# One transfer per quad and per stored tile, two stores for the last tile, and another table of product counts, in a fused attention and feed-forward kernel

## The chip, the cores and the metric

The kernel runs on one core of a Trainium2 chip. The metric is device time in microseconds (us) of one execution; lower is better. In the profile, PE is the matrix engine (PEld its weight loads), ACT the scalar engine, DVE the vector engine, POOL the general engine, and SP the engine that here only issues transfers; SPq, ACTq and POOLq are the queues of transfer instructions that SP, ACT and POOL issue. Sixteen DMA engines move the data of all these queues.

## The reference

Eight batches, 12 heads, 448 positions of 64 numbers. Queries and keys are divided by their norms, attention is taken with a temperature of 0.1, and the result, laid out as 3584 tokens of 768 numbers, goes through a feed-forward layer with `h * cos(h)` between its two products.

```
q_n = q / (norm(q, axis=-1) + 1e-06)
k_n = k / (norm(k, axis=-1) + 1e-06)
scores = q_n @ k_n.transpose(0, 1, 3, 2) / tau          # tau = 0.1
attn = softmax(scores)
x = (attn @ v).transpose(0, 2, 1, 3).reshape(3584, 768)
h = x @ w_in                                            # 768 x 2048
out = (h * cos(h)) @ w_out                              # 2048 x 768
```

Inputs and output are float32. The kernel gives its matrix products bfloat16 operands.

## The kernel before

**Quads and batches.** Attention is done in 24 quads; a quad is four heads of one batch, so three quads (numbers 3b, 3b+1, 3b+2) make batch b. For a quad, `load_qk` brings Q and K in (SP), `square` and `inverse` take the inverse norms, `scale` divides (POOL or DVE), and `turn` transposes Q and K with two transfers (SP). `scores` makes 7 groups of score products (line 549), ACT takes their exponentials (line 556), and `attend` multiplies them with V (line 566). The sum over the keys is applied afterwards. For quads 6 to 23 this goes two quads at a time, in what the code calls a round (`ROUNDS`, `sums`, `invert`): PE sums the exponentials of both quads (line 629), ACT takes the logarithm and the negative exponential of the sums (lines 645 and 647), which leaves eight distinct rows of 448 inverse sums, and ACT sends these eight rows to a scratch tensor in memory, `rscr` (line 648). SP then fetches them back, spread over partitions, into a tile `R` (line 654): for each quad two transfers, one for partitions 0 to 63 and one for 64 to 127. Every partition of a half receives the same 896 numbers. POOL multiplies the attention result with `R` and writes the bfloat16 tile `xT` (line 657). `R` has two buffers, used in turn by quads.

**Batch products.** When the three quads of a batch are in `xT`, PE makes the first product of the feed-forward layer, 96 matrix instructions (`m1_part`, line 675); ACT and DVE apply `h * cos(h)` (`m1`, lines 688 to 694). Then follow the second products of the output tiles that this batch completes (`m2`, line 703). A tile t is 128 tokens; there are 28 tiles. Each has two halves of 384 columns, 16 instructions each; DVE copies each half to `osb` (line 711), which has three buffers, and after the second half SP stores the tile with two transfers, of partitions 0 to 63 and of 64 to 127 (line 717). A token's place in the output is such that the 64 tokens of a half stand 7 rows apart, and the two halves start one row apart, except in tiles 3, 10, 17 and 24, whose halves belong to different batches.

**Order.** Between the second products, the attention work of later batches is put in: `VISITS` lists, for each batch, pairs (slots of attention to do, second products to do after them), and `LATER` shifts the place of a quad's `attend` among its slots. PE executes in the order in which the code creates its operations. The other engines' order comes from `Planner`, which runs through a list of estimated durations once, at build time, and emits a fixed order for each engine; a transfer's estimate is `dur` on its issuing engine and `moves` for the data. Up to quad 3 (`P.strict`) the order of ACT, DVE and POOL is the order of creation. SP issues its transfers strictly in that emitted order, and an instruction that has to wait holds up those behind it.

Of the kernel before, what the change touches and what calls it, by code (L numbers as in the profile page):

```python
# [16 lines left out]
class Op:  # L17
    __slots__ = ("i", "eng", "dur", "fn", "reads", "writes", "deps", "dma", "lat", "start", "end",
                 "count", "waits", "known", "prio", "moves", "mode", "chain", "behind", "lead", "packet", "lock")


class Planner:
# [20 lines left out]
    def op(self, eng, dur, fn, r=(), w=(), after=(), dma=None, moves=0, mode="f", chain=None, keep=False, lead=0.0,  # L43
           packet=74, lock=False):
        o = Op()
        o.i, o.eng, o.dur, o.fn, o.dma, o.moves, o.mode, o.chain = (
            len(self.ops), eng, dur, fn, dma, moves, mode, chain)
        o.lat = self.FIRST + moves + self.LAST if dma else self.LAT[eng]
        o.behind, o.lead, o.packet, o.lock = None, lead, packet, lock
        if keep or self.strict and eng in ("act", "dve", "pool"):  # L50
            o.behind, self.tail[eng] = self.tail.get(eng), o
# [29 lines left out]

    PASSES, SPREAD = 0, 1.5

    def plan(self):

        rng = random.Random(1)
        shift = [0.0] * len(self.ops)
        least = max(o.end for o in self.pass_(shift))
        for _ in range(self.PASSES):
            n = rng.choice((8, 30, 100))  # L90
            i = rng.randrange(len(shift) - n)
            tried = list(shift)
            for k in range(i, i + n):
                tried[k] += rng.gauss(0.0, self.SPREAD)
            end = max(o.end for o in self.pass_(tried))
            if end <= least:
                least, shift = end, tried
        self.order = self.pass_(shift)
        return self.order

    def pass_(self, shift):
# [11 lines left out]
        t, urge = 0.0, [1e9] * len(ops)  # L113
        for o in ops:
            if o.eng == "pe":
                urge[o.i] = t
                t += o.dur
        later = None
        behind = {}
        for o in reversed(ops):  # L120
            if o.eng == "pe":
                if later is not None:
                    urge[o.i] = min(urge[o.i], urge[later.i] - o.dur)
                later = o
            if o.chain:
# [7 lines left out]
        for o in ops:  # L133
            o.prio = (urge[o.i] if urge[o.i] < 1e8 else 2000.0 + o.i) + shift[o.i] - o.lead
        pe = [o.i for o in ops if o.eng == "pe"]
        pe_next = 0
# [138 lines left out]
def bass_cosine_attention__then__act_gcu_kernel(  # L275
# [42 lines left out]
    sqk = sb("sqk", [128, 2 * NJ, D], BF16)  # L318
    n2 = ring("n2", 2, [128, 4 * NJ], F32)
    nrm = ring("nrm", 2, [128, 4 * NJ], F32)  # L320
    rr = ring("rr", 2, [128, 4 * NJ], F32)
    ne = ring("ne", 2, [128, 4 * NJ, 2], F32)
    Qn = ring("Qn", 1, [128, NJ, 2, D], BF16)
# [38 lines left out]
    for i in range(2):  # L362
        op("dve", 0.1, lambda e, i=i: e.memset(ne[i].ap()[:, :, 1], 1e-6), w=[("eps", i)])

# [65 lines left out]

    def jr(t, w, part, off=0):
        return bass.AP(t, off + w * H + part[0], [[2 * H, 128], [NJ, 2], [1, part[1] - part[0]]])

    def square(qd, w, eng, part=ALL[0], after=()):
# [15 lines left out]
        def add():  # L450
            return op("dve", 0.07 + 0.95 * n, lambda e: e.tensor_reduce(  # L451
                out=n2[u].ap()[:, H * w:H * w + H] if part == ALL[0] else jr(n2[u], w, part),
                in_=dst, axis=AX.X, op=ALU.add),
                r=cut("sq" + nm, 0, part), w=cut("n2%d" % w, u, part))
# [3 lines left out]
    def inverse(qd, w0, w1, part=ALL[0], after=()):  # L458
# [5 lines left out]
        if part == ALL[0]:  # L464
            n = slice(H * w0, H * w1)
            t, z, o = n2[u].ap()[:, n], nrm[u].ap()[:, n], rr[u].ap()[:, n]
        else:
            t, z, o = (jr(a[u], w0, part) for a in (n2, nrm, rr))
        act("exp", 0.12, lambda e: e.activation(z, t, ACT.Ln, bias=1e-30, scale=1.0),
# [3 lines left out]
        if qd == 0:  # L473
# [5 lines left out]
            return  # L479
        two_ = ne[u].ap()[:, H * w0:H * w1]  # L480
        act("exp", 0.12, lambda e: e.activation(two_[:, :, 0], z, ACT.Exp, bias=0.0, scale=0.5), r=x, w=[("ne", u)],
# [5 lines left out]
        op("dve", 0.3, lambda e: e.reciprocal(o, z), r=x, w=y, lead=lead)  # L487

    def scale(qd, w, eng="pool", part=ALL[0]):
        s, u = qd % 3, qd % 2  # L490
        j0, j1 = part
        f, n, nm = ((Qf, Qn, "Q"), (Kf, Kn, "K"))[w]
        rb = bass.AP(rr[u], w * H + j0, [[2 * H, 128], [NJ, 2], [1, j1 - j0], [0, D]])
        return op(eng, (1.05 if eng == "dve" else 1.65) * (j1 - j0) / NJ,
# [14 lines left out]

    def transpose(qd, which, bk, part=ALL[0]):  # L510
        u = qd % 3
# [3 lines left out]
        def mm(e):  # L515
# [6 lines left out]
        src = PS.ap()[:, 512 * bk + 64 * j0:512 * bk + 64 * j1].bitcast(BF16)  # L522
        dst = t[u].ap()[:, j0:j1].rearrange("p j a x -> p (j a x)")
        op("dve", 0.07 + 0.067 * (j1 - j0), lambda e: e.tensor_copy(dst, src), r=whole(bk),  # L524
           w=cut(nm + "T", u, part))
# [112 lines left out]
    def invert(quads, bk):  # L638
# [8 lines left out]
        act("exp", 0.47, lambda e: e.activation(zz, zz, ACT.Exp, bias=0.0, scale=-1.0), r=[("Zs", z)], w=[("Zs", z)], lead=LEAD)  # L647
        op("act", 0.3, lambda e: e.dma_start(rscr.ap()[8 * n:8 * n + rows, :], Zs[z].ap()[0:32 * np_:16, :]),
           r=[("Zs", z)], w=[("rs", n)], dma=("rs", z), moves=0.05, lead=LEAD)
        for i, qd in enumerate(quads):  # L650
            u, sl, b = qd % 2, qd % NA, qd // QB
            for r in range(2):
                ap = bass.AP(rscr, (8 * n + 4 * i + 2 * r) * S, [[0, 64], [S, 2], [1, S]])
                op("sp", 0.6, lambda e, r=r, u=u, ap=ap: e.dma_start(R[u].ap()[64 * r:64 * r + 64], ap),
                   r=[("rs", n)], w=[("R", u, r)], dma=("R", u, r), moves=0.85, packet=140, lead=LEAD)
            c0 = 2 * (qd % QB)
            op("pool", 2.04, lambda e, u=u, sl=sl, b=b, c0=c0: e.tensor_tensor(  # L657
                xT[b % 2].ap()[:, c0:c0 + 2, :], AVs[sl].ap(), R[u].ap(), ALU.mult),
                r=[("AV", sl), ("R", u, 0), ("R", u, 1)], w=[("x", b % 2, qd % QB)], lead=LEAD, lock=True)

# [36 lines left out]
    def m2(t, h, f0, f1, bk):  # L697
# [11 lines left out]
        if f1 == NNB:  # L709
            so = t % 3  # L710
            op("dve", 0.475, lambda e: e.tensor_copy(osb[so].ap()[:, HW * h:HW * h + HW], bank(bk, HW)),  # L711
               r=whole(bk), w=[("o", so, h)])
# [10 lines left out]
    VISITS = [  # L723
# [7 lines left out]
        [],  # L731
        [],
    ]
    LATER = {19: 3, 10: -1, 18: -2, 5: 3, 4: 1, 17: 4, 7: -1, 21: -2, 22: -1, 15: -2, 9: 1}
    E1, E2 = NNB - 6, NNB - 4
# [319 lines left out]
```

## Time and profile before

| | us |
| --- | --- |
| median of three runs | 425.83 (425.01 to 428.05) |
| the profiled execution, its own time | 424.88 |
| its span, from the first to the last instruction | 423.0 |
| PE busy | 406.1 |
| ACT busy | 306.3 |
| DVE busy | 269.5 |
| POOL busy | 200.9 |

The profiled execution ran at the full granted clock (1.00). Its time is 1.88 us more than its span. Stretches that the text uses, from the start of the span: the first product of batch 2 starts at 149.6, that of batch 4 at 245.8, that of batch 7 at 379.7, and the last matrix instruction ends at 418.8. In the groups of the page, a row gives line, engine, operation, destination and source tile, sizes and count, then the busy time and the mean of one instruction, then the idle time of the engine ahead of it. The section on transfers gives the count, the size and the median time from issue to landing. The section on queues gives packets, bytes and the time the packets took as a share of sixteen engines over the span.

### The profile page before, as it was taken

The page shows a single profiled execution, that of the slowest core. Times are in us where ns is not written, and L with a number is a line of the kernel's source. Part 1 is how long each engine was busy: PE and PEld are TensorE (multiplying, and loading weights), DVE is VectorE, ACT ScalarE, POOL GpSimd, SP SyncE. Part 2 cuts the span into 40 slices and gives each one's busy share as a digit, 9 for nine tenths or more (in the row PEclk, how much of TensorE's full clock was granted, in tenths as well). Part 3 has the DMA queues.
Part 4 walks back from the last instruction along what each step waited for, and adds up shares of the span by engine and source line. Part 5 has one row for each costly group of instructions (what it writes and reads, how often), then busy time and mean ns, then how long its engine had stood idle before and what let it go on. Part 6 is the DMA issues. An engine that isn't in the chain of part 4 may idle for free.

```text
span 423.0 us, 8441 instructions
## 1 busy us (share of the span) xinstructions
PE 406.1 (96%) x3586; PEld 212.6 (50%) x3586; DVE 269.5 (64%) x337; ACT 306.3 (72%) x404; POOL 200.9 (47%) x137
## 2 busy tenths in 40 slices
PE   6879998999999999999999999999999999999995
PEld 5345454445544445445555555445554555555563
DVE  5767886879853659733996269824882228736921
ACT  6998689988888977697787677689678656505700
POOL 3566238792387794758628880559213213000000
PEclk9999999999999999999999999999999999999999
DMA  8999997995099969298909990279805523021022
GB/s 272 259 236 209 242 273 165 186 218 135 4 220 227 283 107 251 67 238 212 229 5 211 206 279 2 52 179 177 166 1 82 128 72 92 2 74 39 0 76 74
DMA packets 68230, 62.94 MB, mean 149 GB/s; under 512 B 39961, under 2 KB 60769, under 8 KB 68193
## 3 DMA queue, kind: packets, MB, share of 16 engines
q1 hardware_dynamic: 57808, 50.48, 48.3%
q0 software_dynamic: 10240, 11.80, 16.8%
q8 instruction: 28, 0.46, 0.5%
q10 hardware_dynamic: 144, 0.13, 0.1%
q14 instruction: 10, 0.07, 0.0%
HBM read 53.87 MB, written 11.14 MB: 154 GB/s over the span
## 4 chain that ended last, share of the span: by engine, by line
PE 77%; DMA 12%; ACT 4%; DVE 3%; POOL 2%; issue 0%; ACTq 0%; SPq 0%
PE PS L703 30%; PE PS L675 30%; PE PS L566 7%; PE PS L549 6%; DMA W<-in_moe_w_out_dram 6%; PE PS L629 3%; DMA Kf<-in_k_dram 3%; ACT E L556 2%; DMA R<-rscr 1%; DVE n L451 1%; PE PS L588 1%; DMA rscr<-Zs 1%; DMA Qf<-in_q_dram 1%; DVE osb L711 1%; POOL xT L657 0%
## 5 line engine op out<-in xcount | busy, mean ns | idle before, releaser
L556 ACT ACTIVATE E<-PS 128x896 bf16<-128x896 f32 x168 | 142.4, 919 | 20.8 <-PE PS L549 18.4
L703 PE MATMUL PS<-W,gT 128*128 128x384 bf16 x896 | 157.0, 327 | 0.0
L675 PE MATMUL PS<-xT,W 128*128 128x448 bf16 x768 | 147.0, 353 | 1.3 <-DVE qT L524 1.0
L703 PEld LDWEIGHTS PS<-W,gT 128*128 128x128 bf16 x896 | 82.9, 98 | 69.8 <-issue 15.9
L675 PEld LDWEIGHTS PS<-xT,W 128*128 128x128 bf16 x768 | 74.7, 98 | 71.7 <-DVE qT L524 1.1
L688 ACT ACTIVATE ar<-PS 128x896 int32<-128x896 f32 x64 | 58.2, 911 | 37.5 <-PE PS L675 37.5
L690 DVE SCALAR_TENSOR_TENSOR ar<-ar,PS 128x896 f32<-128x896 int32 x64 | 69.2, 1083 | 22.3 <-ACT ar L688 22.3
L694 DVE TENSOR_TENSOR gT<-PS,ar 128x896 bf16<-128x896 f32 x64 | 69.5, 1088 | 7.5 <-ACT ar L692 7.1
L692 ACT ACTIVATE ar<-ar 128x896 f32<-128x896 f32 x64 | 60.6, 946 | 18.2 <-DVE ar L690 18.0
L711 DVE COPY osb<-PS 128x384 f32<-128x384 f32 x56 | 31.1, 556 | 61.2 <-PE PS L703 60.5
L657 POOL TENSOR_TENSOR xT<-AVs,R 128x896 bf16<-128x896 f32 x18 | 37.4, 2086 | 49.6 <-DMA R<-rscr 49.6
L549 PE MATMUL PS<-qT,kT 64*64 64x448 bf16 x672 | 49.7, 359 | 5.3 <-ACT E L556 2.8
L447 POOL TENSOR_TENSOR sqq<-Qf 128x896 bf16<-128x896 f32 x22 | 36.9, 1677 | 34.0 <-DVE n L451 14.4
L447 POOL TENSOR_TENSOR sqk<-Kf 128x896 bf16<-128x896 f32 x21 | 36.9, 1756 | 33.2 <-DVE n L451 32.0
L495 POOL TENSOR_TENSOR Qn<-Qf,rr 128x896 bf16<-128x896 f32 x21 | 38.0, 1812 | 24.3 <-DVE rr L487 16.7
L575 DVE COPY AVs<-PS 128x896 f32<-128x896 f32 x21 | 22.8, 1088 | 29.2 <-PE PS L566 29.1
L566 PE MATMUL PS<-E,Vb 64*64 64x448 bf16 x672 | 36.7, 350 | 0.0
L451 DVE TENSOR_REDUCE n<-sqq 128x14 f32<-128x896 bf16 x24 | 25.7, 1072 | 14.3 <-POOL sqq L447 10.2
L549 PEld LDWEIGHTS PS<-qT,kT 64*64 64x64 bf16 x672 | 16.5, 105 | 31.8 <-ACT E L556 12.8
L495 POOL TENSOR_TENSOR Kn<-Kf,rr 128x896 bf16<-128x896 f32 x18 | 30.3, 1685 | 1.8 <-DMA kT<-Kn 1.8
L451 DVE TENSOR_REDUCE n<-sqk 128x14 f32<-128x896 bf16 (+2 forms) x25 | 25.9, 1040 | 5.8 <-POOL sqk L447 5.8
L566 PEld LDWEIGHTS PS<-E,Vb 64*64 64x64 bf16 x672 | 18.8, 107 | 12.7 <-issue 1.9
(45 smaller groups left out, 175.7 us busy)
## 6 DMA issues: line engine op xcount, KB each, us to landing
Qf<-in_q_dram SPq DMA_DIRECT2D x24, 448.0 KB, 5.4
out_dram<-osb SPq DMA_DIRECT2D x56, 192.0 KB, 3.6
Kf<-in_k_dram SPq DMA_DIRECT2D x23, 448.0 KB, 5.9
R<-rscr SPq DMA_DIRECT2D x36, 224.0 KB, 4.5
Vb<-in_v_dram POOLq DMA_DIRECT2D x24, 224.0 KB, 5.7
W<-in_moe_w_in_dram POOLq DMA_DIRECT2D x4, 768.0 KB, 17.7
W<-in_moe_w_out_dram POOLq DMA_DIRECT2D x4, 768.0 KB, 24.4
qT<-Qn SPq DMA_TRANSPOSE x20, 4.1
```

What stands on the lines that cost most here:

```text
L447: op(eng, (1.68 if eng == "pool" else 1.05) * n, lambda e: e.tensor_tensor(dst, src, src, ALU.mult), r=cut(nm + "f", s, part), w=cut("sq" ...
L451: return op("dve", 0.07 + 0.95 * n, lambda e: e.tensor_reduce(out=n2[u].ap()[:, H * w:H * w + H] if part == ALL[0] else jr(n2[u], w, part) ...
L495: lambda e: e.tensor_tensor(n[0].ap()[:, j0:j1].rearrange("p j r d -> p r j d"), f[s].ap()[:, :, j0:j1], rb, ALU.mult),
L549: ins = e.matmul(bank(bs + r, S, 64 * a, 64 * a + 64), kT[u].ap()[64 * r:64 * r + 64, j, a, :], qT[u].ap()[64 * r:64 * r + 64, :, a, :], s ...
L556: act("exp", 0.81, lambda e: e.activation(E[es].ap(), two(bs), ACT.Exp, bias=0.0, scale=INV_TAU), r=pair(bs), w=[("E", es)], chain="E")
L566: ins = e.matmul(bank(bk + a, S, 64 * r, 64 * r + 64), Vb[vs].ap()[64 * a:64 * a + 64, r, j, :], E[es].ap()[64 * a:64 * a + 64, r, :], sta ...
L675: ins = e.matmul(bank(bk + i2), W1.ap()[:, i, 128 * nb:128 * nb + 128], xT[c % 2].ap()[:, i, :], start=(i == 0), stop=(i == NKC - 1))
L688: op("act", 0.815, lambda e: e.activation(ar[s].ap().bitcast(I32), two(bk), ACT.Identity, bias=0.25, scale=INV2PI), r=bs, w=[("ar", s)])
L690: op("dve", 1.005, lambda e: e.scalar_tensor_tensor(ar[s].ap(), ar[s].ap().bitcast(I32), -2.0 * math.pi, two(bk), ALU.mult, ALU.add), r=bs ...
L692: act("sin", 0.86, lambda e: e.activation(ar[s].ap(), ar[s].ap(), ACT.Sin, bias=GUARD * math.pi / 2.0, scale=GUARD), r=[("ar", s)], w=[("a ...
L694: op("dve", 1.01, lambda e: e.tensor_tensor(gT.ap()[:, 2 * pr:2 * pr + 2, col:col + S], two(bk), ar[s].ap(), ALU.mult), r=bs + [("ar", s)] ...
L703: ins = e.matmul(bank(bk, HW), gT.ap()[:, f, col:col + 128], W2.ap()[:, f, HW * h:HW * h + HW], start=(f == 0), stop=(f == NNB - 1))
```

## The change

1. The inverse sums of a quad are fetched with one transfer instead of two. The source is described as 2 blocks, each read 64 times, of 896 numbers; the destination is the whole 128-partition tile.
2. A stored tile goes out in one transfer instead of two, where both halves lie in one batch: the destination is described as 2 blocks of 64 rows of 768 numbers. Tiles 3, 10, 17 and 24 keep their two transfers. Tile 27, the last, is stored in two transfers by columns: each of 2 blocks of 64 rows of 384 numbers, as soon as that half is copied.
3. `VISITS` and `LATER` have other numbers.
4. In the planner's list, the estimates of the `rscr` transfer are 0.57 and 0.6 (were 0.3 and 0.05), that of the merged fetch 1.9 (was 0.85 for a half), that of a merged store 1.1 (was 0.55 for a half).
5. The small tiles `n2`, `nrm`, `rr` and `ne`, two buffers each, become one tile with a buffer dimension. The planner's search loop (which ran zero passes) is removed; a table `MOVE`, which is empty, and a sort key are added. Two new code paths, `inverse_two` and a copy on ACT in `transpose`, are not called.

```diff
         for i, qd in enumerate(quads):
             u, sl, b = qd % 2, qd % NA, qd // QB
-            for r in range(2):
-                ap = bass.AP(rscr, (8 * n + 4 * i + 2 * r) * S, [[0, 64], [S, 2], [1, S]])
-                op("sp", 0.6, lambda e, r=r, u=u, ap=ap: e.dma_start(R[u].ap()[64 * r:64 * r + 64], ap),
-                   r=[("rs", n)], w=[("R", u, r)], dma=("R", u, r), moves=0.85, packet=140, lead=LEAD)
+            ap = bass.AP(rscr, (8 * n + 4 * i) * S, [[2 * S, 2], [0, 64], [S, 2], [1, S]])
+            op("sp", 0.6, lambda e, u=u, ap=ap: e.dma_start(R[u].ap(), ap),
+               r=[("rs", n)], w=[("R", u)], dma=("R", u), moves=1.9, packet=140, lead=LEAD)
...
-            if h:
-                for sg in range(2):
-                    b, cc = divmod(128 * t + 64 * sg, S)
-                    dst = bass.AP(out.tensor, (S * b + cc // 64) * KM, [[NJ * KM, 64], [1, KM]])
-                    op("sp", 0.6, lambda e, sg=sg, dst=dst: e.dma_start(dst, osb[so].ap()[64 * sg:64 * sg + 64, :]),
-                       r=[("o", so, 0), ("o", so, 1)], w=[("out", t, sg)], dma=("store", so, sg), moves=0.55, packet=121)
+            if end:
+                store(t, HW * h, HW * h + HW, [("o", so, h)])
+            elif h:
+                store(t, 0, KM, [("o", so, 0), ("o", so, 1)])
+
+    def store(t, x0, x1, parts):
+        so = t % 3
+        b, cc = divmod(128 * t, S)
+        n = 2 if cc + 64 < S else 1
+        for sg in range(0, 2, n):
+            b, cc = divmod(128 * t + 64 * sg, S)
+            dst = bass.AP(out.tensor, (S * b + cc // 64) * KM + x0, [[KM, n], [NJ * KM, 64], [1, x1 - x0]])
+            src = osb[so].ap()[64 * sg:64 * (sg + n), x0:x1]
+            op("sp", 0.6, lambda e, dst=dst, src=src: e.dma_start(dst, src), r=parts, w=[("out", t, sg, x0)],
+               dma=("store", so, x0, sg), moves=0.55 * n * (x1 - x0) / KM, packet=121)
...
     VISITS = [
-        [(0, 25), (3, 12), (3, 11), (3, 6), (3, 0), (3, 10), (3, 12), (3, 5), (3, 5), (3, 0), (3, 4), (3, 4), (1, 1)],
...
-        [(0, 24), (3, 8), (3, 14), (3, 10), (3, 20), (3, 16), (3, 24), (3, 10), (3, 0)],
...
+        [(0, 25), (3, 12), (3, 10), (3, 6), (3, 2), (3, 10), (3, 12), (3, 4), (3, 5), (3, 0), (3, 4), (3, 3), (1, 0)],
...
+        [(0, 21), (3, 8), (3, 16), (3, 10), (3, 10), (3, 12), (3, 34), (3, 10), (3, 5)],
...
-    LATER = {19: 3, 10: -1, 18: -2, 5: 3, 4: 1, 17: 4, 7: -1, 21: -2, 22: -1, 15: -2, 9: 1}
+    LATER = {19: 3, 10: -2, 18: -2, 5: 3, 4: 1, 7: -2, 21: -2, 15: -2, 9: 1, 23: 2, 17: 4, 14: 1, 22: -1}
```

More of the change, by code (lines that the diff above doesn't have):

```diff
@@ L18 @@
     __slots__ = ("i", "eng", "dur", "fn", "reads", "writes", "deps", "dma", "lat", "start", "end",
-                 "count", "waits", "known", "prio", "moves", "mode", "chain", "behind", "lead", "packet", "lock")
+                 "count", "waits", "known", "prio", "moves", "mode", "chain", "behind", "lead", "packet", "lock", "key")
 class Planner:
@@ L49, in op @@
         o.behind, o.lead, o.packet, o.lock = None, lead, packet, lock
+        o.key = o.i + (self.MOVE.get(o.i, 0) if self.strict else 0)
         if keep or self.strict and eng in ("act", "dve", "pool"):
-            o.behind, self.tail[eng] = self.tail.get(eng), o
+            self.tail.setdefault(eng, []).append(o)
         o.reads, o.writes = tuple(r), tuple(w)
@@ L80, in land @@
         return s + took + self.LAST
-    PASSES, SPREAD = 0, 1.5
+    MOVE = {}
     def plan(self):
[L86 to L98, printed above, removed]
+        for line in self.tail.values():
+            line.sort(key=lambda o: o.key)
+            for a, b in zip(line, line[1:]):
+                b.behind = a
+        self.order = self.pass_([0.0] * len(self.ops))
         return self.order
@@ L113, in pass_ @@
         t, urge = 0.0, [1e9] * len(ops)
[L114 to L118, printed above, removed]
+        pe = [o.i for o in sorted((o for o in ops if o.eng == "pe"), key=lambda o: o.key)]
+        for i in pe:
+            urge[i] = t
+            t += ops[i].dur
+        later = dict(zip(pe, pe[1:]))
         behind = {}
         for o in reversed(ops):
[L121 to L124, printed above, removed]
+            if o.i in later:
+                urge[o.i] = min(urge[o.i], urge[later[o.i]] - o.dur)
             if o.chain:
@@ L134, in pass_ @@
             o.prio = (urge[o.i] if urge[o.i] < 1e8 else 2000.0 + o.i) + shift[o.i] - o.lead
-        pe = [o.i for o in ops if o.eng == "pe"]
         pe_next = 0
@@ L318, in bass_cosine_attention__then__act_gcu_kernel @@
     sqk = sb("sqk", [128, 2 * NJ, D], BF16)
[L319 to L322, printed above, removed]
+    n2 = sb("n2", [128, 2, 4 * NJ], F32)
+    nrm = sb("nrm", [128, 2, 4 * NJ], F32)
+    rr = sb("rr", [128, 2, 4 * NJ], F32)
+    ne = sb("ne", [128, 2, 4 * NJ, 2], F32)
     Qn = ring("Qn", 1, [128, NJ, 2, D], BF16)
@@ L429, in bass_cosine_attention__then__act_gcu_kernel, with jr @@
     H, NLEAD = 2 * NJ, 5.0
-    def jr(t, w, part, off=0):
-        return bass.AP(t, off + w * H + part[0], [[2 * H, 128], [NJ, 2], [1, part[1] - part[0]]])
+    def jr(t, u, w, part):
+        return bass.AP(t, (2 * u + w) * H + part[0], [[4 * H, 128], [NJ, 2], [1, part[1] - part[0]]])
     def square(qd, w, eng, part=ALL[0], after=()):
@@ L451, in add @@
             return op("dve", 0.07 + 0.95 * n, lambda e: e.tensor_reduce(
-                out=n2[u].ap()[:, H * w:H * w + H] if part == ALL[0] else jr(n2[u], w, part),
+                out=n2.ap()[:, u, H * w:H * w + H] if part == ALL[0] else jr(n2, u, w, part),
                 in_=dst, axis=AX.X, op=ALU.add),
@@ L465, in inverse @@
             n = slice(H * w0, H * w1)
-            t, z, o = n2[u].ap()[:, n], nrm[u].ap()[:, n], rr[u].ap()[:, n]
+            t, z, o = n2.ap()[:, u, n], nrm.ap()[:, u, n], rr.ap()[:, u, n]
         else:
-            t, z, o = (jr(a[u], w0, part) for a in (n2, nrm, rr))
+            t, z, o = (jr(a, u, w0, part) for a in (n2, nrm, rr))
         act("exp", 0.12, lambda e: e.activation(z, t, ACT.Ln, bias=1e-30, scale=1.0),
@@ L487, in inverse, with inverse_two @@
         op("dve", 0.3, lambda e: e.reciprocal(o, z), r=x, w=y, lead=lead)
+    def inverse_two():
+        flat = "p u n -> p (u n)"
+        t, z, o = (a.ap().rearrange(flat) for a in (n2, nrm, rr))
+        c2, x, y = ([c for u in range(2) for w in range(2) for c in cut("%s%d" % (k, w), u, ALL[0])] for k in ("n2", "nrm", "rr"))
+        both = ne.ap().rearrange("p u n i -> p (u n) i")
+        act("exp", 0.17, lambda e: e.activation(z, t, ACT.Ln, bias=1e-30, scale=1.0), r=c2, w=x)
+        act("exp", 0.17, lambda e: e.activation(both[:, :, 0], z, ACT.Exp, bias=0.0, scale=0.5), r=x,
+            w=[("ne", 0), ("ne", 1)])
+        op("dve", 0.2, lambda e: e.tensor_reduce(out=z, in_=both, axis=AX.X, op=ALU.add),
+           r=[(k, u) for k in ("ne", "eps") for u in range(2)], w=x)
+        op("dve", 0.55, lambda e: e.reciprocal(o, z), r=x, w=y)
     def scale(qd, w, eng="pool", part=ALL[0]):
@@ L508, in norm_b, with transpose @@
         return last
-    def transpose(qd, which, bk, part=ALL[0]):
+    def transpose(qd, which, bk, part=ALL[0], eng="dve"):
         u = qd % 3
@@ L523, in transpose @@
         dst = t[u].ap()[:, j0:j1].rearrange("p j a x -> p (j a x)")
+        if eng == "act":
+            op("act", 0.13 + 0.067 * (j1 - j0), lambda e: e.activation(dst, src, ACT.Copy), r=whole(bk), w=cut(nm + "T", u, part))
+            return
         op("dve", 0.07 + 0.067 * (j1 - j0), lambda e: e.tensor_copy(dst, src), r=whole(bk),
@@ L647, in invert @@
         act("exp", 0.47, lambda e: e.activation(zz, zz, ACT.Exp, bias=0.0, scale=-1.0), r=[("Zs", z)], w=[("Zs", z)], lead=LEAD)
[L648 to L649 removed]
+        op("act", 0.57, lambda e: e.dma_start(rscr.ap()[8 * n:8 * n + rows, :], Zs[z].ap()[0:32 * np_:16, :]),
+           r=[("Zs", z)], w=[("rs", n)], dma=("rs", z), moves=0.6, lead=LEAD)
         for i, qd in enumerate(quads):
             u, sl, b = qd % 2, qd % NA, qd // QB
[L652 to L655 removed]
+            ap = bass.AP(rscr, (8 * n + 4 * i) * S, [[2 * S, 2], [0, 64], [S, 2], [1, S]])
+            op("sp", 0.6, lambda e, u=u, ap=ap: e.dma_start(R[u].ap(), ap),
+               r=[("rs", n)], w=[("R", u)], dma=("R", u), moves=1.9, packet=140, lead=LEAD)
             c0 = 2 * (qd % QB)
```

9 lines of the change are left out of this document (5 added, 4 removed), and 10 rows, old and new, of the table VISITS.

## The prediction

> **What bounds the kernel now.** I read the page's engine row, then the busy time by stretch, then the waits of PE, the chain of work, and last the transfers. Engines and queues of the whole span, from the page:
>
> ```profile
> PE 406.1 (96%) x3586; PEld 212.6 (50%) x3586; DVE 269.5 (64%) x337; ACT 306.3 (72%) x404; POOL 200.9 (47%) x137
> ...
> q1 hardware_dynamic: 57808, 50.48, 48.3%
> ...
> q10 hardware_dynamic: 144, 0.13, 0.1%
> ```
>
> PE is the bound. By stretches it is busy 83.54 of the 86 us from 64 to 150, 95.56 of 96 up to 246, 133.74 of 134 up to 380. So 3.16 us of idle time are left between 64 and 380. The rest of PE's 17 idle us lie in the start, whose PE order the change leaves alone, and in the 4.2 us after the last matrix instruction. The DMA engines (share of sixteen) stand in the same stretches, without PE:
>
> ```profile
> 64.00:150.00 86.00, 1.00 0.80 179
> 150.00:246.00 96.00, 1.00 0.76 174
> 246.00:380.00 134.00, 1.00 0.44 98
> 380.00:423.00 43.00, 1.00 0.18 46
> ```
>
> The fourth column is the DMA share: the sixteen engines together are four fifths busy up to 246. The chain of work shows where a transfer meets PE, here ahead of batch 2:
>
> ```profile
> 137.05 4.43 DMA rscr<-Zs
> 141.50 0.48 SPq L654
> 142.01 5.41 DMA R<-rscr
> 147.49 2.09 POOL xT L657
> 149.63 16.82 PE PS L675 x88
> ```
>
> PE waits only 0.3 us for `xT` there, so the fetch of `R` is on the path with no slack; before the other batches the last `xT` (POOL's timeline) ends some 4 to 6 us ahead of PE's first product. Last, over how many engines a transfer goes. From the transfer view of 380 to 423, where nothing but stores runs, and the page's row of the eight-row transfer:
>
> ```profile
> DMA packets 802, 2.00 MB, mean 46 GB/s; under 512 B 160, under 2 KB 160, under 8 KB 800
> ...
> out_dram<-osb SPq DMA_DIRECT2D x10, 192.0 KB, 2.7
> ```
>
> ```profile
> rscr<-Zs ACTq DMA_DIRECT2D x9, 14.0 KB
> ```
>
> Ten stores of 64 rows make 640 data packets (3072 B) and 160 small ones: 16 each, one from every engine at its end. The queue q10 carries only the nine `rscr` transfers of eight rows: 144 packets less 72 rows leave 72 small ones, 8 each. So a transfer is dealt out by rows, and one of eight rows used eight engines; its rows were not cut to fill sixteen.
>
> **The change, part by part.**
>
> *The fetch and the store: how many engines.* Before, every description that SP issues begins with a count of 64 or 128. After, the fetch's source begins with 2 blocks, and a merged store's destination begins with 2 blocks of 64. If the dealing goes by that outermost count, as the eight-row transfer suggests, the merged transfers run on two engines, 64 packets each, and two engines carry what sixteen carried. The rows alone don't exclude that all 128 rows are counted; I take the outermost count. The Trainium skill, page "DMA: Bandwidth & Descriptors", section "Why a DMA increments its semaphore by 16 and not by 1", states it: the engine count is the largest number up to 16 that divides the slowest dimension (other than 1) of both sides, and "Rules for kernel authors" there warns of a leading broadcast dimension. The eight-row transfer agrees; no run of before shows a leading 2. The same page also advises one 128-partition transfer over two halves; by that sentence alone the sum would be the first rival's.
>
> *Price of a merged transfer.* By the packet records of the trace, an `R` packet (3584 B) takes 140 ns in its quickest quarter and 226 on the mean, a store packet (3072 B) 121 at best; the mean by the transfer view of the last two stores (80.3% of 1.9 us for 8 packets per engine) is 190. The long ones come in bursts that all sixteen share, at about twice the short ones; with two engines I take the short ones. A fetch then holds each of the two engines 64 x 0.140 = 8.96 us (at most 14.5), a store 64 x 0.121 = 7.74 us (at most 12.2). Before, a half fetch cost each engine 0.90 us and a half store 0.69. All SP transfers share one queue per engine, so loads and transposes wait behind these, and the two engines set the pace. I make their ledger by stretch: the DMA share times the length, less the present fetches and stores, is the other traffic on each engine. It can be as low as three quarters of that, since its packets have short values too (256 B: 18 ns against a mean of 28; 1792 B: 74 against 89); I take the middle, 0.875.
>
> - 64 to 150: other 0.80 x 86 - 8 x 0.90 - 12 x 0.69 = 53.3, taken 46.7. Fetches for quads 6, 7, 8: 26.9. Stores of tiles 0, 1, 2, 4, 5: 38.7; tile 3 as before, 1.4. Sum 113.7 in 86 us: **+28** (21 to 34).
> - 150 to 246 (batches 2 and 3, which need quads 9 to 11 and 12 to 14): other 0.76 x 96 - 12 x 0.90 - 14 x 0.69 = 52.5, taken 45.9. Six fetches 53.8, stores of 6 to 9 and 11 38.7, tile 10 1.4. Sum 139.8 in 96: **+44** (37 to 50).
> - 246 to 380: other 0.44 x 134 - 16 x 0.90 - 20 x 0.69 = 30.8, taken 26.9. Nine fetches (15 to 23) 80.6; tiles 12 to 16, 18 to 20 61.9; tile 17 1.4. Sum 170.8 in 134: **+37** (33 to 41).
> - From 380: no fetch is left, PE runs its 39 us as before, but tiles 25 to 27 leave PE every 5.2 us (twice 16 products at 0.163 us; the chain has 128 of them in 20.81) and take 7.74. Tile 25 starts at about 410 and ends at 418; 26 ends at 425.6; the halves of 27 (half a store, 3.9 each) at 429.4 and 433.3. Before, the last data packet ended at 422.2: **+11**.
>
> In these orders SP's queue is nearly never empty on the two engines, since two quads' transposes and loads stand behind each round; where SP waits for an `osb` of the next batch first, the gap adds a few us to this, which I leave to the range.
>
> *Issues.* SP issues 51 fetches and stores where it issued 92, at a median of 0.59 us. That frees 24 us of SP, which idled for `osb` (120 us): nothing on the path but one issue ahead of the batch-2 fetch and one at the end, together 1.1 us at most, and the two engines swallow both. The new `store` waits for one copy less for tile 27; behind SP's waits stand loads and transposes, as before. POOL's multiply (2.09 us) holds up squares and scales behind it on POOL while it waits for `R`, now longer; PE has them on its path two quads later, by which time the fetch is the later one.
>
> *The table.* Product counts per batch stay the same; only their places move. The gain can't exceed PE's 3.16 idle us. The largest squeeze, in batch 3 (20 and 16 products become 10 and 12), leaves PE 10 x 0.163 + 3 x 0.23 = 2.3 us between groups for which ACT needs 3 x 0.92 = 2.8; the three pairs of banks cover half a microsecond. Between -3.2 and +3: I take 0, and with PE no longer the bound either end is cover.
>
> *Tiles in one, planner, unused paths.* The same instructions on the same data; an empty table and equal keys; the order of PE is unchanged up to the second visit of batch 0. Zero: no instruction is added. The changed estimates only choose an order, priced with the table.
>
> Sum against the profiled execution, 424.88: + 28 + 44 + 37 + 11 = 545. (It stands 0.95 below the median of the three runs, which is nothing here.) One per cent, 4.3 us, is about what a measurement tells from no change.
>
> **The rivals.**
>
> *All sixteen engines after all* (the 128 rows are dealt out): against it stand the eight packets of the eight-row transfer, for it that a count of blocks is not a count of rows. A fetch stays at 8 rows per engine, about 1.8 us; the end saves one issue (0.5), the table 0 to 3.2, a wait may cost 1: 421 to 426, say **424**, not slower. It decides if the merged store leaves 16 small packets. Chance 0.08 within 1%, 0.02 faster by more (the table gaining its whole 3.2 and the end its 0.5 doesn't quite reach 4.3).
>
> *Only the stores fall on two engines*, as the fetch is dealt by its destination, whose count is 128. The ledger of the three stretches with fetches at 1.8 us per quad: 46.7 + 5.4 + 40.1 = 92, 45.9 + 10.8 + 40.1 = 97, 26.9 + 16.2 + 63.3 = 106, against 86, 96 and 134: +6, +1, 0 and the end's +11: **443**. Chance 0.05.
>
> *Two engines, but each packet at its mean* (226 and 190 ns): 18 fetches add 18 x 5.5 = 99, 23 stores 23 x 4.4 = 101: **745**. For it: most `R` packets took over 200; against it: these lie in bursts on sixteen engines. It is the far end of the forecast's case; I give 0.05 to more than 640.
>
> **How the numbers follow.** Forecast 545, chance 0.80 on two engines below 640. Range 500 to 640: below, the first stretch's backlog not felt (-28) and the other traffic at its short packets (-17); above, the middle between short and mean packets (+100). Left out: the first two rivals and the far end, 0.20. Slower by over 1%: 0.80 + 0.05 + 0.05 = 0.90; within 1% 0.08; faster 0.02.
>
> **What would show it.** Right: the transfer rows give `R<-rscr` x18 at 448 KB with 11 us or more to landing (4.5 now) and merged stores with 9 or more; the small packets of the queue fall to 2 for each; the DMA share drops though the span grows; POOL's waits for `R` and PE's waits for `xT` grow to tens of us, PE's first products start some 28, 72 and 109 us later in batches 2, 4 and 7; the last copy ends some 14 us before the end, not 3.7. Wrong: 16 small packets for each merged store, and landings near 5 us.

## The result, and the profile after

The changed kernel takes **581.79 us** in the median (578.45 to 589.35, 6 runs); the kernel before, beside it, 426.91 (425.01 to 428.68, 6 runs). The ratio is **1.361**, interval 1.354 to 1.368. The forecast was 545, the range 500 to 640. The profiled execution took 578.45 us, its span 576.5.

From the page of the changed kernel, the engines, the DMA share in 40 slices, SP's queue, and the rows of the transfers (a row without a last number has no landing time):

```profile
PE 436.1 (76%) x3586; PEld 219.8 (38%) x3586; DVE 268.9 (47%) x337; ACT 308.5 (54%) x404; POOL 198.3 (34%) x137
...
DMA  9999998855951869649517995099642211111021
...
q1 hardware_dynamic: 56678, 50.47, 48.1%
...
out_dram<-osb SPq DMA_DIRECT2D x23, 384.0 KB
R<-rscr SPq DMA_DIRECT2D x18, 448.0 KB
...
qT<-Qn SPq DMA_TRANSPOSE x20, 8.3
```

PE is no longer the bound: it is busy 30 us longer (406.1 before) and idle 140 us where it idled 17; 30 + 123.5 make the 153.5 us of span that were added. The bytes of the queue are the same. Who keeps PE and POOL waiting, from the two views of waits (us in total, times, longest), and the same wait of POOL in the kernel before:

```profile
PE PS L679 <- POOL xT L661: 51.8, 8, 13.2
PE PS L554 <- DMA kT<-Kn: 26.5, 4, 19.2
PE PS L679 <- DVE gT L698: 16.6, 4, 13.1
```

```profile
POOL xT L661 <- DMA R<-rscr: 205.0, 18, 22.0
```

```profile
POOL xT L657 <- DMA R<-rscr: 49.6, 11, 14.0
```

All 18 multiplies of POOL wait for their fetch now, 11 did before. In the chain of work, ahead of batches 2 and 7 (start, length, what):

```profile
168.21 21.89 DMA R<-rscr
...
192.29 18.71 PE PS L679 x88
...
479.00 30.83 DMA R<-rscr
...
521.08 18.17 PE PS L679 x88
...
560.08 0.56 DVE osb L716
```

The fetch that took 5.41 us ahead of batch 2 takes 21.89; ahead of batch 7 it is on the path with 30.83. How many engines carry this is best seen where SP's queue holds nothing but fetches and stores. The transfer view from 475 to 560 us, in 40 slices of 2.1 us:

```profile
DMA  1111111111111111111111111111111000441111
GB/s 56 51 51 51 50 52 53 52 53 60 52 53 51 54 51 51 51 51 51 51 52 52 52 60 52 52 52 52 52 52 52 3 0 0 97 98 29 46 52 52
```

For 66 us on end the share stands at one tenth (two engines of sixteen are 0.125) and the rate at 50 to 54 GB/s in all slices but three (56 to 60). Two engines at one fetch packet (3584 B) per 140 ns would give 51. The packet records of the trace say the same: from 475 to 541 exactly two packets are in flight for 61 of the 66 us. At 547, behind the gap, the two halves of tile 24 go first, over sixteen engines, and the rate goes to 97.

By stretches of the changed kernel, cut where PE's first product of batches 2, 4 and 7 starts (after the early pair of its first tile); the columns are the bounds, the length, the busy time of PE, PEld, DVE, ACT and POOL, the granted clock, the DMA share and GB/s:

```profile
64.00:192.30 128.30, 88.98 (x880) 43.41 (x878) 60.04 (x75) 78.08 (x104) 58.46 (x38) 0.87 0.67 117
192.30:355.00 162.70, 116.67 (x876) 56.15 (x876) 66.31 (x81) 77.81 (x100) 71.09 (x46) 0.84 0.75 112
355.00:521.00 166.00, 136.24 (x1044) 67.75 (x1044) 73.43 (x87) 85.81 (x106) 38.83 (x24) 0.91 0.39 68
521.00:576.50 55.50, 38.97 (x216) 21.44 (x216) 21.25 (x24) 14.16 (x16) 0.02 (x1) 0.87 0.14 48
```

The products of batch 4 begin at 332.6 by PE's timeline (the rest of them follow at 355.1, after a wait for `gT`), so the first products start 42.7, 86.8 and 141.4 us later than before in batches 2, 4 and 7.

### The profile page after: what moved, and what is told of

It reads as the page before. It is cut to its first block, busy times and chain, and to the rows that moved or that the text cites. A ratio compares the mean times of both kernels' runs of the same rounds, so it can differ in the third digit from the quotient of the medians.

```text
span 576.5 us, 8382 instructions
## 1 busy us (share of the span) xinstructions
PE 436.1 (76%) x3586; PEld 219.8 (38%) x3586; DVE 268.9 (47%) x337; ACT 308.5 (54%) x404; POOL 198.3 (34%) x137
## 3 DMA queue, kind: packets, MB, share of 16 engines
q1 hardware_dynamic: 56678, 50.47, 48.1%
## 4 chain that ended last, share of the span: by engine, by line
DMA 46%; PE 21%; POOL 12%; issue 10%; DVE 4%; SPq 2%; ACT 2%; POOLq 0%
DMA R<-rscr 23%; PE PS L679 12%; DMA qT<-Qn 6%; PE PS L707 6%; DMA Kf<-in_k_dram 6%; DMA rscr<-Zs 5%; DMA W<-in_moe_w_out_dram 5%; POOL xT L661 4%; POOL Qn L497 2%; POOL sqk L436 2%; POOL sqq L436 2%; POOL Kn L497 1%; DMA Qf<-in_q_dram 1%; DVE n L440 1%; SPq L536 1%
## 5 line engine op out<-in xcount | busy, mean ns | idle before, releaser
L679 PE MATMUL PS<-xT,W 128*128 128x448 bf16 x768 | 165.0, 379 | 69.3 <-POOL xT L661 51.8
L707 PE MATMUL PS<-W,gT 128*128 128x384 bf16 x896 | 162.3, 334 | 0.0
L679 PEld LDWEIGHTS PS<-xT,W 128*128 128x128 bf16 x768 | 78.2, 104 | 154.4 <-POOL xT L661 44.2
L707 PEld LDWEIGHTS PS<-W,gT 128*128 128x128 bf16 x896 | 84.5, 99 | 74.2 <-issue 23.0
L661 POOL TENSOR_TENSOR xT<-AVs,R 128x896 bf16<-128x896 f32 x18 | 37.3, 2074 | 205.0 <-DMA R<-rscr 205.0
L696 ACT ACTIVATE ar<-ar 128x896 f32<-128x896 f32 x64 | 60.6, 947 | 42.9 <-DVE ar L694 42.7
L554 PE MATMUL PS<-qT,kT 64*64 64x448 bf16 x672 | 51.8, 369 | 36.3 <-DMA kT<-Kn 26.5
L497 POOL TENSOR_TENSOR Qn<-Qf,rr 128x896 bf16<-128x896 f32 x21 | 36.4, 1732 | 36.1 <-DMA qT<-Qn 27.7
L554 PEld LDWEIGHTS PS<-qT,kT 64*64 64x64 bf16 x672 | 16.5, 106 | 64.7 <-issue 38.7
L634 PE MATMUL PS<-E,sel 128*32 128x448 bf16 x252 | 14.9, 379 | 13.6 <-DVE osb L716 13.3
```

What stands on the lines that cost most here:

```text
L497: lambda e: e.tensor_tensor(n[0].ap()[:, j0:j1].rearrange("p j r d -> p r j d"), f[s].ap()[:, :, j0:j1], rb, ALU.mult),
L554: ins = e.matmul(bank(bs + r, S, 64 * a, 64 * a + 64), kT[u].ap()[64 * r:64 * r + 64, j, a, :], qT[u].ap()[64 * r:64 * r + 64, :, a, :], s ...
L679: ins = e.matmul(bank(bk + i2), W1.ap()[:, i, 128 * nb:128 * nb + 128], xT[c % 2].ap()[:, i, :], start=(i == 0), stop=(i == NKC - 1))
L696: act("sin", 0.86, lambda e: e.activation(ar[s].ap(), ar[s].ap(), ACT.Sin, bias=GUARD * math.pi / 2.0, scale=GUARD), r=[("ar", s)], w=[("a ...
L707: ins = e.matmul(bank(bk, HW), gT.ap()[:, f, col:col + 128], W2.ap()[:, f, HW * h:HW * h + HW], start=(f == 0), stop=(f == NNB - 1))
```

## The experiments

**Which part costs the time.** Three kernels, each the changed one with one or both merged transfers cut in halves again, as before; table, planner and the column halves of the last tile stay as changed. The first has this edit to the fetch and to the store:

```diff
-            ap = bass.AP(rscr, (8 * n + 4 * i) * S, [[2 * S, 2], [0, 64], [S, 2], [1, S]])
-            op("sp", 0.6, lambda e, u=u, ap=ap: e.dma_start(R[u].ap(), ap),
+            for r in range(2):
+                ap = bass.AP(rscr, (8 * n + 4 * i + 2 * r) * S, [[0, 64], [S, 2], [1, S]])
+                op("sp", 0.6, lambda e, r=r, u=u, ap=ap: e.dma_start(R[u].ap()[64 * r:64 * r + 64], ap),
...
-        n = 2 if cc + 64 < S else 1
+        n = 1
```

> The changed kernel with its fetches and its stores cut again into transfers of 64 rows (36 fetches; two stores per tile, and for the last tile two per column half); the new table, the last tile's early half and all else stay. Theory (merged transfers run on two of sixteen DMA engines, and these set the pace): back to 421 to 427 us, 16 small packets for each transfer. Rival (the new table or order costs the time): stays above 440. In between: both have a share.

The second halves the fetch alone and keeps the merged stores:

> The changed kernel with the fetches cut again into halves of 64 rows, the stores left merged. Theory: 2 small packets for each merged store, 16 for each fetch; the ledger of the prediction gives 443 us (435 to 455), the last 11 us of it after PE is done. Rival (the fetch alone, being on PE's path, costs the time): 421 to 428.

The third halves the stores alone and keeps the merged fetch:

> The changed kernel with the stores cut again into halves of 64 rows, the fetches left merged. Theory: the two engines have room (82 of 86 us, 109 of 96, 121 of 134 by the ledger), so the cost is the later landing of the second fetch of a round, some 12 us, less 4 to 6 us of slack, in batches 2, 3 and 5, and 13 us of overload: 440 to 460. The extra times of this run and of the one with merged stores then add up to clearly less than the 155 us of both together, as each alone finds the engines with room. Rival (costs of separate waits that simply add): the two sum to about 155.

Measured: both in halves 428.39 us, ratio 1.0135 (1.008 to 1.020); only the stores merged 484.70, ratio 1.1425 (1.140 to 1.146); only the fetch merged 492.91, ratio 1.162 (1.159 to 1.165). So the merged transfers are the whole of the loss but for a per cent. In units of the kernel before, the merged stores alone add 12.9% to the halves, the fetch alone 14.8%, both together 34.8%: more than the sum, as the third expectation had it. Each alone cost more than expected, though: 484.70 for 435 to 455, and 492.91 for 440 to 460. SP's queue on the three pages, in this order:

```profile
q1 hardware_dynamic: 57968, 50.48, 48.3%
```

```profile
q1 hardware_dynamic: 57218, 50.47, 52.6%
```

```profile
q1 hardware_dynamic: 57428, 50.47, 48.8%
```

The count of packets tells the engines. Data packets are the same in all of them, so a difference is one of small packets at the ends of transfers. From halves to merged stores 50 transfers become 25, and 750 packets go: 50 x 16 - 25 x 2. From halves to merged fetch 36 become 18, and 540 go: 36 x 16 - 18 x 2. With both (56678) 1290 go: 86 x 16 - 43 x 2. So every merged transfer uses two engines, the one whose source begins with 2 as well as the one whose destination does. Why each alone cost more than its ledger is taken up below.

**How many engines are enough.** The fetch stays one transfer per quad, but its source begins with 4 or 16 blocks instead of 2. For that the sums of the two heads are written alternately and all 128 rows go to scratch (224 KB per `rscr` transfer instead of 14); the stores are in halves.

```diff
-        e.memset(sel.ap()[0:64, 0:16], 1.0)
-        e.memset(sel.ap()[0:64, 16:32], 0.0)
+        e.memset(sel.ap()[0:64, 0:32:2], 1.0)
+        e.memset(sel.ap()[0:64, 1:32:2], 0.0)
...
-            ap = bass.AP(rscr, (8 * n + 4 * i) * S, [[2 * S, 2], [0, 64], [S, 2], [1, S]])
+            ap = bass.AP(rscr, (128 * n + 64 * i) * S, [[4 * S, 16], [0, 8], [S, 2], [1, S]])
```

> Stores in halves of 64 rows; one fetch per quad, its source described as 4 blocks read 32 times each instead of 2 blocks read 64 times. For that the sums are left with the two heads interleaved and all 128 rows (not 8) go to the scratch tensor. Theory: 4 engines, 32 packets each at 0.144 us, 4.6 us a fetch; 4 small packets a fetch; 424 to 436 us. Rival (the merged fetch costs by its single wait, not by its engines): as with 2 blocks.

> The same with 16 blocks read 8 times each: theory, 16 engines, 8 packets each, 16 small packets a fetch, landing near 5 us, 420 to 428 us, so that one fetch per quad by itself costs nothing. Rival (single wait): as with 2 blocks. The write of 128 rows instead of 8 may cost up to 1 us ahead of a round.

Measured: 4 blocks 459.39 and 452.53 us (two runs, the first profiled), 16 blocks 427.00 us (10 runs, 424.88 to 430.77), ratio 1.0057 (1.003 to 1.009). From the page of the 16 blocks:

```profile
q1 hardware_dynamic: 57680, 50.48, 49.2%
...
R<-rscr SPq DMA_DIRECT2D x18, 448.0 KB, 6.1
```

Against the halves 288 small packets are gone, 36 x 16 - 18 x 16: sixteen engines. With 4 blocks 504 are gone (57464), 36 x 16 - 18 x 4: four. On 2, 4 and 16 engines the same 18 fetches give 492.9, 452.5 (the better of the two runs) and 427.0 us. With 16 blocks the merged fetch costs nothing against both in halves (428.39), so it isn't the merging that costs but the small outermost count. The 4 blocks were expected at 424 to 436 and took 16 to 23 us more than the top of that. A fetch holds four engines for 32 x 0.14 = 4.5 us each, 81 us in all, so they are far from full. The chain of the profiled run shows what was left out: the two fetches of a round come at once, 9.0 us for four engines, and the chain has such fetches four times, with 9.35, 17.50, 10.28 and 10.54 us. So, as far as that chain shows, it is the wait for a landing that costs here, not the amount of work; no run takes it apart further.

**Both on sixteen.** The store, too, as one transfer over sixteen engines: the scores read their queries in token order, so that a tile's 128 rows lie in a row in memory.

```diff
-                                   qT[u].ap()[64 * r:64 * r + 64, :, a, :],
+                                   qT[u].ap()[64 * r:64 * r + 64, :, a, :].rearrange("p j x -> p x j"),
...
-            dst = bass.AP(out.tensor, (S * b + cc // 64) * KM + x0, [[KM, n], [NJ * KM, 64], [1, x1 - x0]])
+        dst = bass.AP(out.tensor, 128 * t * KM + x0, [[KM, 128], [1, x1 - x0]])
```

> One fetch per quad in 16 blocks and one store per tile on sixteen engines: the score products read the queries in token order (a strided read of PE's moving operand), so that a tile's 128 tokens are 128 consecutive rows of the output and the store's description begins with 128. All else as changed. Theory: 419 to 425 us. Rival: PE pays for the strided read; the 672 score instructions are some 34 us of PE at 0.05 each, and at half speed this run is at 450 or more.

Measured 508.46 us, ratio 1.195 (1.191 to 1.200). The transfers did what was wanted, but PE is busy for 498.8 us; from its page, and below it the score products of the kernel before:

```profile
L554 PE MATMUL PS<-qT,kT 64*64 64x448 bf16 x672 | 141.0, 922 | 0.9 <-DVE kT L529 0.9
...
out_dram<-osb SPq DMA_DIRECT2D x27, 384.0 KB, 2.5
```

```profile
L549 PE MATMUL PS<-qT,kT 64*64 64x448 bf16 x672 | 49.7, 359 | 5.3 <-ACT E L556 2.8
```

A score product takes 922 ns where it took 359 with the queries in their own order: its moving operand now steps 256 B from element to element. The Trainium skill, page "Advanced Engine Details and Errata", section "SBUF Cachelines", says that SBUF has lines of 16 bytes and that a different line per access is penalised; this row agrees and gives the price, a factor of 2.6.

**The stores from another issuer.** The changed kernel with its merged stores issued by ACT, so that they have a queue of their own and SP's loads and transposes don't stand behind them.

```diff
-            op("sp", 0.6, lambda e, dst=dst, src=src: e.dma_start(dst, src), r=parts, w=[("out", t, sg, x0)],
+            op("act", 0.57, lambda e, dst=dst, src=src: e.dma_start(dst, src), r=parts, w=[("out", t, sg, x0)],
```

> The changed kernel with all stores issued by ACT instead of SP, same descriptions: still two engines, but in another queue, so that loads and transposes no longer stand behind stores in SP's queue. Theory (the work of the two engines is the bound): 560 to 590, as now. Rival (the time beyond the ledger, some 33 us, is SP held up while its queue on the two engines is full): 535 to 555.

Measured 610.94 us, ratio 1.440 (1.433 to 1.447): slower than the changed kernel, and outside both expectations. The same transfers are to be moved, and SP is hardly freer: its loads, transposes and fetches took it 245 us to issue, 261 in the changed kernel. The largest of its waits in this run:

```profile
SPq L536 <- POOL Qn L497: 119.9, 11, 34.1
```

SP's transposes wait 120 us for POOL's `Qn`, 38 in the changed kernel, and POOL in its order waits 225.8 us for the fetch, 205.0 there. So the second queue freed nothing. Why the run is slower still than the changed kernel, no run shows.

**Without the transposes on the queue.** In the changed kernel, the issue of one transpose takes SP up to 18 us, against a mean of 1.5 before. To see whether they are the bottleneck, quads 5 to 23 are transposed by PE instead, as quads 0 to 3 are already; once on the kernel with halves (the control), once on the changed one.

```diff
         if qd + 2 < NQ:
             norm_b(qd + 2)
-            turn(qd + 2)
...
+        if FIRST + 1 < qd + 1 < NQ:
+            bk = next_pair()
+            for w in range(2):
+                transpose(qd + 1, w, bk + w)
```

> Control for the next run: the changed kernel with fetches and stores in halves of 64 rows, and the queries and keys of quads 5 to 23 transposed on PE (line 519, with copies on DVE) instead of by 38 of the 40 transfers of SP. PE gets some 19 x 0.8 = 15 us more work: 435 to 455 us in all theories.

> The changed kernel with its merged transfers on two engines, and the same transposes on PE. Theory (the time beyond the ledger is SP held in transpose instructions, whose data stand behind the merged transfers; 147 us of SP in the changed kernel against 61 before): without them the ledger by stretches, with 2.6 us a quad less of other traffic, gives +12, +26, +21 and +11, some 60 to 85 us above the control. Rival 1 (any transfer is held when the queue of the two engines is full): 95 to 115 above the control. Rival 2 (transposes play no part): about 150 above it.

Measured: the control 449.83 us, ratio 1.055; the changed kernel with it 578.80, ratio 1.358 (1.351 to 1.365). Merged transfers cost 129 us here. My theory said 60 to 85 and fell, and neither rival's range holds the figure (95 to 115, and about 150). 34,000 of the 35,840 packets of the transposes were gone, and the time stayed. SP's timeline in this run, around the fetch ahead of batch 2:

```profile
136.11 1.17 SPq L658 DMA_DIRECT2D R<-rscr  x2
138.63 16.52 SPq L388 DMA_DIRECT2D Qf<-in_q_dram  x1
```

Now a plain load is held for 16.52 us. So it is not the transpose as such: a load behind a round's two fetches is held as well. The two engines need 18 us for them (256 packets at 0.14 us over two engines), and the longest holds, 16.52 here and 18.15 for a transpose in the changed kernel, are about that long; behind other rounds they are 7 to 13 us.

**The table alone.** The kernel before with only `VISITS` and `LATER` of the change.

```diff
-    LATER = {19: 3, 10: -1, 18: -2, 5: 3, 4: 1, 17: 4, 7: -1, 21: -2, 22: -1, 15: -2, 9: 1}
+    LATER = {19: 3, 10: -2, 18: -2, 5: 3, 4: 1, 7: -2, 21: -2, 15: -2, 9: 1, 23: 2, 17: 4, 14: 1, 22: -1}
```

> The kernel before with the new table of product counts and shifts alone. Theory: within 1 per cent of the kernel before, 421 to 428. Rival (the table alone costs what the run in halves showed above the kernel before, ratio 1.0135): 427 to 432.

Measured 431.93 us, ratio 1.0123 (1.007 to 1.017): the table alone loses about 5 us, where I had taken 0 and 3 at most. This is outside the expectation and within the rival. With the estimates and the column halves beside it, in the first experiment, it is 1.0135, in the one with 16 blocks 1.0057: about a per cent that is not the transfers'.

**The kernel before with the good half of the change.** Its own table, one fetch per quad on 16 engines, the last tile by columns, stores in halves.

> The kernel before, with its own table: one fetch per quad in 16 blocks, stores in halves of 64 rows, the last tile's column halves stored apart. Theory: 423 to 426; the end one issue shorter at best, the fetch neither better nor worse. Rival (one fetch per quad helps by issues saved): 420 or less.

Measured 429.29 us, ratio 1.0075 (1.004 to 1.011), 3 us above the top of the expectation. Nothing here beats the kernel before; the fetch on 16 engines lands in 5.9 us in one piece, where its halves landed in 4.5. Which of its edits costs the 0.75% is not shown.

## Why the prediction was right, and where it was off

**Two engines: right.** It was taken from one row, the eight-row transfer with eight small packets, against the rival that 128 rows are dealt out. The packet counts say 2 for every merged transfer, 4 and 16 for 4 and 16 blocks, and the plateau of 51 GB/s says the same without counting. The Trainium skill's rule, page "DMA: Bandwidth & Descriptors", section "Why a DMA increments its semaphore by 16 and not by 1" (the largest number up to 16 that divides the slowest dimension of both sides), holds in all of these. The rivals "all sixteen" and "only the stores on two" are gone: the merged fetch alone costs 14.8%.

**The price of a packet: right.** Taken were 140 and 121 ns, the quickest quarter; the packet records of the changed kernel give means of 147 (3584 B, the fetches) and 139 ns (3072 B, all stores but the last tile's). The rival at the mean of before, 226 and 190, is out. The mean of a fetch packet grows with the engines that a fetch uses, 147, 175 and 221 ns on 2, 4 and 16, which fits the argument that the long ones share a rate.

**The ledger of the two engines: right; that they are never idle: wrong.** The sum took a stretch to last as long as the two engines have work. From the packet records one can count how long SP's queue had no packet in flight. They don't name the engine, so a time in which other engines than the two moved something counts as work. In the table, us; the kernel with merged stores alone is added, with the ledger that the second rival made for it:

| stretch | ledger | measured length | queue empty | length less empty |
|---|---|---|---|---|
| changed, up to batch 2 | 113.7 | 128.3 | 17.3 | 111.0 |
| changed, up to batch 4 | 139.8 | 140.3 | 9.3 | 131.0 |
| changed, up to batch 7 | 170.8 | 188.4 | 18.9 | 169.5 |
| stores merged, up to batch 2 | 92 | 109.9 | 17.2 | 92.7 |
| stores merged, up to batch 4 | 97 | 107.3 | 18.0 | 89.3 |
| stores merged, up to batch 7 | 106 | 146.7 | 40.2 | 106.5 |

The work was priced within 3% in four of six rows and 7 to 9% too high in the other two; what was missing is the empty time. The fetch merged alone gives the same: up to batch 7 its ledger was 312 (82, 109 and 121), the length less the empty time is 313.9, and 70.7 us were empty. The prediction's step is the sentence that SP's queue is nearly never empty on the two engines and that a gap where SP waits for an `osb` adds a few us. It adds 9 to 19 per stretch, 45 in all; the middle stretch, +44.1 for +44, came out right only because its ledger was 9 too high. The five longest gaps of the changed kernel, by stretch of time (columns as in the table of stretches above):

```profile
113.40:124.40 11.00, 11.00 (x98) 5.85 (x97) 9.83 (x13) 9.35 (x12) 3.25 (x3) 1.00 0.02 1
299.20:305.00 5.80, 1.99 (x24) 0.91 (x28) 2.55 (x3) 1.26 (x3) 5.78 (x5) 0.50 0.29 40
365.50:377.00 11.50, 11.35 (x112) 5.86 (x111) 10.81 (x15) 7.96 (x13) 4.59 (x4) 1.00 0.17 22
450.90:455.40 4.50, 3.34 (x23) 1.71 (x21) 1.11 (x2) 3.45 (x4) 4.50 (x3) 1.00 0.01 4
541.00:548.00 7.00, 7.00 (x45) 4.21 (x43) 4.08 (x6) 0.98 (x2) 0.00 (x0) 1.00 0.01 2
```

In three of them PE is fully busy at full clock, in the other two POOL is, and SP's transfers stand still (what DMA share is left is of other queues). SP's waits put the first down to a store that waits for its `osb`, 15.5 us. But the transposes behind that store could not have gone any earlier. From the chain of work, and from SP's timeline:

```profile
118.95 1.09 DVE gT L698
120.04 1.00 DVE n L440
...
123.53 1.70 POOL Qn L497
```

```profile
125.26 1.52 SPq L536 DMA_TRANSPOSE qT<-Qn  x1
```

DVE comes to the sums `n` of the next quad's squares only behind the `gT` of the batch's first product, POOL waits 15.0 us for them, and the transpose goes 0.03 us after `Qn` is done. The gap at 365.5 is the same (POOL waits 14.8 us for `n`). In the two in which POOL is busy, POOL has waited for the fetch ahead of its multiply and makes `Qn` only then, and again the transpose goes at once (303.82 after 303.80, 454.18 after 454.14). The prediction named this, POOL's squares and scales held up behind a longer wait, but took the fetch to be the later one all the same and put the rest at nothing. Only in the last gap do the stores alone wait for PE. So the queue is empty where what it is to move next hasn't been made, by a chain that begins at PE's product or at the fetch itself. The bounds take turns instead of overlapping, and the time lies above the larger of the two. The kernel before had such gaps too (16.4 us from 100.9, 21.3 from 252.6, 24 to 78 us per stretch by the packet records); they were its slack, and I counted all of it as room that the two engines would fill. The ledger of the kernel without transposes says the same from the other side: up to batch 7 it stood 77 us empty where the changed one stood 45, and so the lighter queue gained next to nothing.

**By stretch.** +42.7, +44.1, +54.6 and +12.1 us against +28, +44, +37 and +11; the sum is 153.5 of span, forecast 120. The end is right in its working too: the last copy of `osb` ends at 560.64, 16 us ahead of the end (14 foreseen), and the last stores follow it. Batch starts were foreseen 28, 72 and 109 us late and are 43, 87 and 141.

**The table at nothing: wrong; whether it is covered stays open.** Alone it loses 1.2%. How much of that is left in the changed kernel, where PE waits 140 us anyway, no run tells; I had argued that it would be cover.

**Issues at nothing: half right.** No time came from fewer issues, but SP did not become freer: it spent 316 us in issues of transfers, 146 before. I take it, without a run that shows it, that this does not add to the time by itself, since SP is held while the two engines work; it decides what is issued late. Ahead of batch 2 the second round's fetches went out at 168.21, though ACT had issued their `rscr` transfer at 146.54, because SP stood in a transpose. SP's timeline:

```profile
145.03 18.15 SPq L536 DMA_TRANSPOSE qT<-Qn  x1
...
168.21 9.87 SPq L658 DMA_DIRECT2D R<-rscr  x2
```

**What would show it.** Fetches of 12 to 31 us in the chain, two small packets each, waits of POOL and PE: as foreseen. That the DMA share drops is seen in the stretches (0.67, 0.75, 0.39 and 0.14 for 0.80, 0.76, 0.44 and 0.18), but hardly over the span: q1 stands at 48.1% for 48.3. The packets of the transposes lasted longer in the mean, as told at the end.

**What stays open.** The gaps were counted, not taken away; no run shows the changed kernel with a gap removed. So the 45 us are an account that closes, and not the effect of an edit.

## What to carry to other kernels

Count the engines of a transfer by the outermost count of its description on both sides before merging two into one: a leading 2 in fetch and store cost 35% here; in the fetch alone it cost 15%, and a leading 16 in its place nothing that can be told. The small packets at the end of the transfers tell the count from the page alone. When a queue becomes a second bound beside an engine, do not take the larger of the two: look in the old trace for the stretches where the queue is empty because what it is to move next is still being made, and add those to the queue's work.

## What the runs showed of the hardware that was not expected

- An issue on SP is held while earlier transfers fill two of the engines: a load's 0.6 us became up to 8.05 in the changed kernel and 16.5 with the transposes on PE, and a transpose's 1.5 us up to 18.
- While two engines were full, the 256 B packets of the transposes grew from 28 to 69 ns in the mean (27 with halves, 45 with the fetch merged, 54 with the stores merged). The median stayed at 18: few packets make the difference, 349 of over 1 us (122 before), which hold 1,715 of the 2,480 us. While any of these is in flight there are mostly 16 to 20 at once (90 of 103 us), so it is not the two engines alone that are held; by what, no run shows.
- PE's granted clock fell with its waits, to 0.84 to 0.91 by stretch, from 1.00; 88 products took 18.2 to 18.7 us instead of 16.82 (ahead of batch 7 the clock is 0.60 in their first 3.4 us and 1.00 after), and the rows of PE at work in the gaps show 1.00. The Trainium skill, page "TensorE: Matmul & The Clock Gate", section "HAM oscillation — how this bites in real kernels", describes that waits for data lower the clock and the next work starts slow; the rows agree. Ahead of batch 7 this is on the path, 1.35 us.
